# Paired final adds and stores, w1 loaded after all of x, an earlier first spin, and a new rank table in a hedgehog-mixer plus MLP kernel

## The chip, the cores and the metric

The kernel runs on one core of a Trainium2 chip. The metric is the device time of one execution in microseconds, as the median of repeated runs. The engines are TensorE (PE; its weight loads are shown apart as PEld), VectorE (DVE), ScalarE (ACT), GpSimd (POOL) and SyncE (SP). SP computes nothing: it issues nearly all transfers, one after the other.

## The reference, cut to what matters

x is a 2048 x 448 block in bf16 (D = 448, 16 heads of 28, F = 1792).

```python
xn = layernorm(A_x)
# A: linear attention with softmax feature maps
q, k, v = split_heads(xn @ wqkv)
phi(t) = concat(softmax(t @ w_phi), softmax(-(t @ w_phi)))      # per head
o = (phi(q) @ (phi(k).T @ v)) / (phi(q) @ sum_s phi(k) + 1e-6)
A = merge_heads(o) @ wo
# B: token-shift mixer, then an MLP
h  = gelu(layernorm(xn) @ w1)
x1 = xn + concat(4 column blocks of h, shifted by +1, -1, +2, -2 rows) @ w2
B  = x1 + gelu(layernorm(x1) @ w3) @ w4
return A_x + A + B
```

B_x is not read: both branches work on xn.

## The kernel before

The 2048 rows are 16 tiles of 128 rows; tile i holds row `res_of(i)` of each group of 16, so neighbours in time are neighbouring tiles. Everything stays in SBUF. PSUM is four slots of two banks each (pool `ps`); each matmul group takes a slot until it is copied out.

The program is not written in its final order. `P.add(name, engine, cost, rank, deps, emit, uses)` adds a task, and `Planner.run` (L245) lays all tasks out by list scheduling: among the tasks that could start about now on an engine, the one with the lowest rank goes first. The ranks come from a table of text, `RANKS` (L366), read by `set_ranks` (L351); a number after `@` is an earliest start. `Planner.run` also holds an estimate of how long loads take: a task with a negative `lag` waits in one line behind the earlier loads. `Recorder` (L17) then turns the order into one instruction stream for each engine and works out which waits each instruction needs. So a changed rank or cost can move any instruction of any engine, but never changes what is computed. All VectorE and GpSimd work has line L209, all activations L205, matmuls L197, transposes on PE L201, plain transfers L212 and transposing transfers L215.

The tasks, in the order of the work, with the names used below:

- Loads on SP, in the order the table gives: `x0`, `x1`, `x2` (2 tiles), `x4`, `x8`, `x12` (4 tiles each, 448 KB); `wk`, `wq`, `wv`, `w1` in pieces of 336 and 56 KB (L586 to L637). ACT issues `phi`.
- `z_kvq` (L689): seven VectorE memsets of `kvq`. `spin0` to `spin19` (L730): twenty matmuls of 240 columns on `kvq`, whose result nobody reads; each can start when `z_kvq` is done.
- LayerNorm of tile i on VectorE: `st` (statistics), `ag`, `sc..e`, then `sc` on POOL (the power), `ap` (apply) and `du` (a copy of 64 columns).
- `xT0` to `xT3`: tiles 0 to 3 transposed on PE, copied out by `xTc0` to `xTc3`. Tiles 4 to 15 are transposed by transfers `xD4` to `xD15` on SP, each after its `du`.
- `wTk`, `wTq`: 16 transposes each of the K and Q weights, copied out by `wTck0/1`, `wTcq0/1`; then `foldk0/1`, `foldq0/1` multiply them by w_phi, copied out by `foldck0/1` and `foldcq0/1` on ACT.
- `Vj`, `Kj` (j = 0 to 7, two tiles each, 14 matmuls of 448 columns in two parts, a with 8 and b with 6) and `Qn` (n = 0 to 7, 14 matmuls of 512). Each K and Q is followed by two exponentials on ACT (`.e0`, `.e1`), each V by a copy (`.e`) on ACT or VectorE. `red`, `rec`, `nrm` normalise phi(k).
- `W1j` and four `gel` (Gelu) tasks per j on ACT, after the table load behind `warm2`. `nudge0/1` and `put6` to `put9` move four blocks across the edge of the shift. `hDj` (SP) transposes h, `W2j` multiplies by w2, `W2j.r` adds xn; `hD` has three buffers, so hD6, hD5, hD7 wait for W20.b, W21.b, W22.b.
- `kv0` to `kv3`, `kvm`: phi(k).T @ v. `numi` (16 matmuls), `n1` to `n7` and `oDj`: the attention output of tile i, its division and its transpose.
- A second LayerNorm, `gDj` (SP) its transpose, `Hg_f` (g = 0 to 3, f = 0 to 6; 14 matmuls of 512, Gelu `.g` on ACT), and at last `Fp_q`: h3 @ w4 and o @ wo for two tiles, 70 matmuls. `xsi` (POOL) is xn plus x.
- `fini.q` (VectorE) adds `xs` to the F result, `outi.q` stores it (L1237 to L1247): one of each per tile. F7 is cut into two column halves, q = 0 and 1.

Of the kernel before, what the change touches and what calls it, by code (L numbers as in the profile page):

```python
# [366 lines left out]
warm 868.4 tiny 970.5 phi -70.0 x0 -486.0 x1 -79.6 wk0 -291.7 wk1 284.2 x2 326.9 wv0 1117.1 wv1 954.7 wv2 792.3 wq0  # L367
444.5 wq1 375.6 x4 733.3 x8 1139.7 x12 1546.2 w10 640.0 w11 1288.0 w12 1936.1 bdl -321.6 bdh 970.7@5139 mask
1098.4@1625 pick 966.2@4497 ident 958.1@1998 mhalf -318.4 z_h 959.3@1573 nudge 971.2@1597 z_pk -285.0 z_v -272.1 z_wpq
998.3 z_kvq 286.2 st0 853.0 ag0 208.4 sc0e 294.4 sc0 -285.3 ap0 258.7 du0 57.9 st1 204.5 ag1 60.2@4897 sc1e 288.1 sc1  # L370
997.3 ap1 243.1 du1 1112.4 st2 205.2 ag2 227.0 st3 252.9 ag3 294.2 sc2e 1063.7 sc2 970.7 ap2 63.9 ap3 271.9 du2 268.8
st4 84.4 ag4 239.6 st5 239.8 ag5 874.0 sc4e 102.1 sc4 991.8 ap4 286.4 ap5 495.5 du4 65.4 st6 287.4@11185 ag6 865.4 st7
239.4@11166 ag7 156.1 sc6e 205.0 sc6 971.2@13677 ap6 157.0 ap7 220.7 du6 90.4 st8 28.7@13523 ag8 243.2@16614 st9
288.9@13637 ag9 413.8 sc8e -323.1 sc8 1243.7 ap8 782.0@20130 ap9 797.1 du8 1090.5 st10 243.7@13806 ag10 84.0 st11
259.2@13643 ag11 205.1 sc10e 244.0 sc10 986.2 ap10 495.3 ap11 156.9 du10 82.0@20186 st12 313.5 ag12 204.3 st13 761.4
ag13 28.6@20784 sc12e 263.1 sc12 1162.8 ap12 176.8 ap13 157.2 du12 369.7 st14 234.9@18290 ag14 305.3@19922 st15
82.9@17719 ag15 228.5@19848 sc14e 313.4 sc14 1188.5@22933 ap14 251.2 ap15 262.1 du14 264.6 f0 1188.9 f8 870.9@24467
xT0 296.7@6540 xT1 589.9@8454 xTc0 769.9@7438 xTc1 829.3 xT2 308.9 xT3 575.0 xTc2 822.2@11260 xTc3 896.9@11975 xD4
463.2 xD5 487.3 xD6 397.4 xD7 480.3 xD8 479.7 xD9 456.4 xD10 490.4 xD11 488.2 xD12 476.1@27407 xD13 425.8@25657 xD14
422.8@28403 xD15 486.3@30159 wTk 278.3 wTck0 872.2 wTck1 847.2 foldk0 291.2@8902 foldck0 873.4 foldk1 290.8@7999  # L380
foldck1 861.1 wTq 597.2@7001 wTcq0 815.4 wTcq1 576.6 foldq0 112.7@9432 foldcq0 873.8@10814 foldq1 309.8 foldcq1
770.5@11650 V0.a 131.0 V0.b 596.4 V0.e 814.9 V1.a 611.2 V1.b 621.0 V1.e -217.9 V2.a 283.7@19412 V2.b 243.7 V2.e 855.1
V3.a 258.1@25132 V3.b 615.5 V3.e 530.1 V4.a 413.8 V4.b 487.7@32840 V4.e 648.6 V5.a 2130.9 V5.b 315.3 V5.e 343.8 V6.a
1092.4 V6.b 656.1 V6.e 491.9 V7.a 1096.5 V7.b 374.4 V7.e -228.4 K0.a 590.7 K0.b 596.7 K0.e0 875.6 K0.e1 507.0 red0
1501.6 rec0 1501.9 nrm0 1188.1 red1 1498.0@21181 rec1 118.3 nrm1 1157.5 K1.a 283.9@17349 K1.b 609.8 K1.e0 509.1 K1.e1
-216.6 red2 786.6 rec2 515.2 nrm2 1160.2 red3 264.5@32297 rec3 290.1 nrm3 1159.4 K2.a 575.7 K2.b 283.4 K2.e0
-202.6@23116 K2.e1 919.1 red4 797.0 rec4 226.8 nrm4 870.8 red5 1498.8 rec5 293.5 nrm5 407.5@40914 K3.a 183.0 K3.b
621.3 K3.e0 828.9 K3.e1 501.7 red6 1377.0 rec6 499.7 nrm6 399.9@33939 red7 516.5@30012 rec7 1379.7 nrm7 1187.7 K4.a
675.4 K4.b 1438.8 K4.e0 729.0 K4.e1 718.7 red8 1533.4 rec8 1413.5 nrm8 390.6 red9 1380.6 rec9 1474.4 nrm9 407.3 K5.a
644.7@37806 K5.b 683.8 K5.e0 496.9 K5.e1 496.4 red10 1439.5 rec10 -331.0 nrm10 403.0 red11 1435.2@50122 rec11  # L390
-297.4@53022 nrm11 415.4 K6.a 401.9 K6.b 644.6 K6.e0 -263.9@34806 K6.e1 501.3@33944 red12 1500.3 rec12 1437.9 nrm12
857.2 red13 1417.4 rec13 1380.5 nrm13 1159.5 K7.a 682.7 K7.b 1126.1 K7.e0 493.7 K7.e1 648.4 red14 307.4 rec14 1462.0
nrm14 1098.5 red15 1418.2 rec15 1474.5 nrm15 407.1 Q0.a 569.0 Q0.b 263.5 Q0.e0 543.6 Q0.e1 543.6 Q1.a 290.1 Q1.b 596.6
Q1.e0 785.1 Q1.e1 522.7 Q2.a 1491.2 Q2.b 261.5 Q2.e0 647.5@28961 Q2.e1 242.8@28196 Q3.a 595.2 Q3.b 242.4 Q3.e0 785.4
Q3.e1 -312.2 Q4.a 175.1 Q4.b 283.7 Q4.e0 904.2@33049 Q4.e1 498.8 Q5.a 355.3 Q5.b 413.2 Q5.e0 499.2 Q5.e1 903.8 Q6.a
594.9 Q6.b 478.9 Q6.e0 492.2 Q6.e1 529.8 Q7.a 1057.0 Q7.b 683.2 Q7.e0 349.0 Q7.e1 660.7 warm2 529.2@45117 W10.a
656.5@43897 W10.b 949.8 gel0.0 728.6 gel0.1 340.6 gel1.0 532.8 gel1.1 744.8 W11.a 804.7 W11.b 213.9 gel2.0 -228.0
gel2.1 658.3 gel3.0 482.7 gel3.1 659.0 W12.a 916.6 W12.b 930.6 gel4.0 349.8 gel4.1 494.5 gel5.0 519.7 gel5.1 482.9
W13.a 1439.6 W13.b 682.4 gel6.0 640.8 gel6.1 725.6 gel7.0 492.4@53544 gel7.1 493.3@52599 W14.a 1446.7 W14.b 1478.5
gel8.0 644.4 gel8.1 372.5 gel9.0 349.8@55542 gel9.1 494.5 W15.a 1073.7@51311 W15.b 525.8 gel10.0 658.6 gel10.1 656.9  # L400
gel11.0 349.9 gel11.1 350.4 W16.a 2141.1 W16.b 1086.0 gel12.0 358.7 gel12.1 492.6@57478 gel13.0 688.0 gel13.1
366.6@57534 W17.a 687.1 W17.b 707.4 gel14.0 491.3 gel14.1 492.1 gel15.0 366.1 gel15.1 -228.4 nudge0 1075.4@59991 put8
505.8@60597 put9 327.7@61558 nudge1 1073.1 put7 492.5 put6 736.9 hD0 177.9 hD1 147.9 hD2 187.5 hD3 194.4 hD4 213.9 hD5
223.0@59251 hD6 199.2 hD7 198.0@59683 kv0 918.8 kv1 1477.9 kv2 1071.3 kv3 882.5 kvc 1430.0 kvm 259.3 kvo0 1803.8 kvo1
1544.6 w20 485.1 w21 419.6 w22 417.3 w23 525.4 W20.a 1446.5 W20.b 1060.2 W20.r 1493.4 st2_0 1438.4 ag2_0 1431.6 st2_1
1535.3 ag2_1 1020.8@59199 sc2_0e 1487.3 sc2_0 409.9@61475 ga0 1036.1 ga1 1450.3@62958 gD0 187.6 W21.a 214.3 W21.b
523.9 W21.r 1464.6 st2_2 1438.2 ag2_2 1488.1 st2_3 1437.9 ag2_3 1464.8 sc2_2e 1556.8 sc2_2 376.0 ga2 1418.4 ga3 1036.5
gD1 162.3 W22.a 525.7 W22.b 525.6 W22.r 1557.2 st2_4 1535.7@63878 ag2_4 1826.3 st2_5 1750.8 ag2_5 909.6@73450 sc2_4e
1470.9@74052 sc2_4 947.9@75836 ga4 1547.5 ga5 1503.7 gD2 148.3 W23.a 497.9 W23.b 524.6 W23.r 1849.7 st2_6 1900.8 ag2_6
1451.3 st2_7 1813.2 ag2_7 1410.1@73193 sc2_6e 1487.6 sc2_6 857.8 ga6 1036.7 ga7 749.0 gD3 157.7 W24.a 297.4@76488  # L410
W24.b 525.9 W24.r 1874.5 st2_8 1416.0 ag2_8 1033.4 st2_9 1529.3 ag2_9 1721.7 sc2_8e 1548.2 sc2_8 666.0 ga8 743.9 ga9
1943.6 gD4 266.5@86330 W25.a 907.3 W25.b 279.2@65249 W25.r 1518.3@67862 st2_10 1906.4 ag2_10 1504.1 st2_11
1545.7@73156 ag2_11 1739.6@75171 sc2_10e 1901.7 sc2_10 872.0 ga10 1813.1 ga11 749.7@85280 gD5 290.3 W26.a 1070.4 W26.b
465.7@63251 W26.r 1813.1 st2_12 1567.0@67359 ag2_12 1825.8 st2_13 1036.4@66877 ag2_13 1885.8@74867 sc2_12e 1826.4
sc2_12 407.8 ga12 1828.6 ga13 1545.9@100527 gD6 1700.4 W27.a 283.9@66012 W27.b 297.5 W27.r 1503.5 st2_14 1419.6 ag2_14
1437.5@71900 st2_15 1825.9@74052 ag2_15 1548.0 sc2_14e 1548.2@82777 sc2_14 925.1 ga14 746.9@95166 ga15 1904.0 gD7
1685.8 w30 419.0 w31 406.5 wo0 423.1 wo1 491.3 wo2 461.4 w4 494.1 num0 466.2 n1_0 1546.3 n2_0 1393.7 n3_0 1760.0@76183
n4_0 749.2 n5_0 1904.7 n6_0 1069.2 n7_0 936.0 num1 525.7 n1_1 1544.5 n2_1 1896.2 n3_1 1470.5@81970 n4_1 1559.1 n5_1
1776.2 n6_1 1813.2 n7_1 927.9@86239 od0 1946.5 oD0 268.1 num2 504.3@83674 n1_2 1526.8@85094 n2_2 1770.0 n3_2 1039.2
n4_2 989.8 n5_2 1778.7 n6_2 1814.1 n7_2 1695.3 num3 541.1 n1_3 1796.4 n2_3 1722.5 n3_3 1957.9 n4_3 1527.3 n5_3 1001.0  # L420
n6_3 1526.9 n7_3 662.7 od1 1896.2 oD1 293.4 num4 551.0 n1_4 752.3 n2_4 1546.2 n3_4 1901.0 n4_4 748.0 n5_4 2206.7 n6_4
1533.1 n7_4 1772.9 num5 557.6 n1_5 751.8 n2_5 2205.0 n3_5 1021.6 n4_5 1512.8 n5_5 1021.8 n6_5 1596.5 n7_5 598.4 od2
1015.6 oD2 1674.3 num6 841.7 n1_6 1513.0 n2_6 723.9 n3_6 1593.5 n4_6 745.4 n5_6 1010.2 n6_6 1594.1 n7_6 663.6@106936
num7 1026.4 n1_7 2207.5 n2_7 1545.8 n3_7 1545.5 n4_7 2209.9 n5_7 744.5 n6_7 1542.2 n7_7 600.2 od3 1884.4 oD3 1734.2
# [29 lines left out]
def bass_parallel_sum__linear_kernel_hedgehog__mixer_s_mlp__prompt_kernel(  # L454
# [18 lines left out]
    with es:  # L473
# [114 lines left out]
        def load(name, dst, src, rank, eng="SP", kb=100.0, after=()):  # L588
            return P.add(name, eng if isinstance(eng, dict) else {eng: 510}, None, rank, after,
                         lambda t: R.dma(dst, src, t.eng), lag=-kb * RATE.get(name, 2.6 if dst.ap[-1][1] > 512 else 3.3))  # L590
# [691 lines left out]
```

The softmax here doesn't subtract the row's maximum and nothing guards it: scores larger than these inputs give would overflow.

## Time and profile before

| | us |
|---|---|
| median of 13 runs | 178.1 (177.1 to 178.84) |
| the profiled execution | 177.1 |
| its span in the profile | 175.4 |
| PE busy in the span | 169.3 (97%), 2080 matmuls |
| DVE, ACT, POOL busy | 115.1, 81.4, 78.9 |
| transfers | 18.30 MB, mean 104 GB/s |

The profiled execution is the fastest of the 13 runs. What lies between its time and its span (1.7 us) is outside the program's instructions. The first 16 spins take 3.38 us, 0.2 us each, and the 16 transposes of `wTk` after them 2.00 us; the same 16 transposes of `wTq`, from 8.06 us on, take 1.20. The tables of the profile give starts and durations in us from the span's start; "L197 PE MATMUL ps<-w,hT" is a matmul that reads w and hT and writes the tile ps.

The order on SP before is x0 wk0 x1 wk1 x2 wq1 wq0 w10 x4 wv2 wv1 wv0 x8 w11 x12 w12, then the transposes xD.

### The profile page before, as it was taken

To read this page: it belongs to the slowest core of one execution; us is meant where nothing else is said; L and a number is where in the kernel's file an instruction comes from. 1 tells how busy PE (TensorE), PEld (TensorE's weight loads), DVE (VectorE), ACT (ScalarE), POOL (GpSimd) and SP (SyncE) were. 2 spreads that over 40 slices of the span, in tenths; PEclk is the share of its full clock that TensorE was granted. 3 is DMA by queue.
4 is the path that set the end of the run, shared out by engine and by line. 5 is a ranking of instruction groups with operands and counts; after the bars stand their busy time and mean duration, and the time that the engine had idled before them with its cause. 6 is when DMAs were issued, how large, how long until landed. Compare 5 with 4: busy or idle time off the path is not lost.

```text
span 175.4 us, 4846 instructions
## 1 busy us (share of the span) xinstructions
PE 169.3 (97%) x2080; PEld 106.2 (61%) x2080; DVE 115.1 (66%) x300; ACT 81.4 (46%) x116; POOL 78.9 (45%) x105
## 2 busy tenths in 40 slices
PE   5999999999999979999999999999999999999993
PEld 4875555555555655455555667655666666766793
DVE  3889999977991898995986655820654554370133
ACT  3399999989999411173657000427001561200000
POOL 7526387699469034035522254630138141261080
PEclk9999999999999999999999999999999999999999
DMA  6994445599909497523054526130010403313022
GB/s 153 260 343 112 74 82 102 113 390 310 322 8 179 89 103 131 104 51 74 4 111 86 106 39 136 53 64 0 0 56 26 90 0 64 60 52 64 0 86 79
DMA packets 41766, 18.30 MB, mean 104 GB/s; under 512 B 33552, under 2 KB 40848, under 8 KB 41744
## 3 DMA queue, kind: packets, MB, share of 16 engines
q1 hardware_dynamic: 41136, 17.91, 43.3%
q8 instruction: 16, 0.26, 0.6%
q10 hardware_dynamic: 608, 0.08, 0.3%
q14 instruction: 6, 0.05, 0.1%
HBM read 8.28 MB, written 1.84 MB: 58 GB/s over the span
## 4 chain that ended last, share of the span: by engine, by line
PE 92%; DMA 5%; DVE 1%; issue 1%; DVEq 0%; SPq 0%
PE ps L197 90%; DMA hT<-hq 3%; PE ps L201 2%; DMA gT<-wv 2%; DVE kvq L209 0%; DVE vaug L209 0%; DVEq L169 0%; SPq L215 0%
## 5 line engine op out<-in xcount | busy, mean ns | idle before, releaser
L205 ACT ACTIVATE phik<-ps 128x1024 bf16<-128x1024 f32 (+1 forms) x44 | 41.3, 997 | 44.7 <-PE ps L197 44.7
L209 DVE TENSOR_TENSOR vaug<-ps,vaug 128x464 f32<-128x464 f32 (+3 forms) x66 | 32.9, 505 | 21.3 <-PE ps L197 15.9
L197 PE MATMUL ps<-w,phik 64*128 64x448 bf16 (+1 forms) x504 | 46.0, 328 | 0.0
L197 PE MATMUL ps<-gT,w 64*128 64x512 bf16 x392 | 44.5, 376 | 0.3 <-DMA gT<-wv 0.3
L197 PEld LDWEIGHTS ps<-w,phik 64*128 64x128 bf16 x504 | 29.5, 94 | 12.2 <-ACT phik L205 0.3
L197 PEld LDWEIGHTS ps<-gT,w 64*128 64x128 bf16 x392 | 22.8, 94 | 17.5 <-DVE vaug L209 0.7
L209 POOL TENSOR_TENSOR xnT<-vaug 128x224 bf16<-128x224 f32 x32 | 17.3, 565 | 27.7 <-DVE vaug L209 27.7
L209 POOL TENSOR_TENSOR vaug<-xn,xtok 128x448 f32<-128x448 bf16 x16 | 16.5, 1039 | 28.6 <-DVE vaug L209 26.4
L209 POOL TENSOR_TENSOR phik<-phik,ksum 128x896 bf16<-128x896 bf16 x14 | 25.0, 1813 | 6.2 <-DVE ksum L209 6.2
L209 POOL TENSOR_TENSOR rs<-rs,mhalf 128x2 f32<-128x2 f32 (+1 forms) x17 | 11.5, 685 | 28.3 <-DVE rs L209 21.1
L205 ACT ACTIVATE eq<-ps 120x1024 bf16<-120x1024 f32 (+1 forms) x18 | 17.5, 1043 | 5.9 <-PE ps L201 5.0
L209 DVE TENSOR_REDUCE ksum<-phik 128x32 f32<-128x896 bf16 x16 | 16.7, 1063 | 1.5 <-ACT phik L205 1.5
L209 DVE RECIPROCAL vaug<-ps 128x16 f32<-128x16 f32 x16 | 4.1, 254 | 19.1 <-PE ps L197 19.1
L197 PE MATMUL ps<-wo,xnT 64*128 64x448 bf16 (+1 forms) x126 | 14.1, 328 | 0.0
L197 PE MATMUL ps<-xnT,hq 64*120 64x512 bf16 x112 | 13.4, 376 | 0.0
L197 PE MATMUL ps<-wv,xnT 64*128 64x448 bf16 x112 | 13.2, 349 | 0.0
L197 PE MATMUL ps<-w,hT 64*128 64x448 bf16 x56 | 12.1, 349 | 1.0 <-DMA hT<-hq 1.0
L197 PE MATMUL ps<-wpk,xnT 64*128 64x448 bf16 x112 | 12.9, 349 | 0.0
L197 PE MATMUL ps<-w2s,hT 64*128 64x448 bf16 x56 | 12.1, 350 | 0.0
L209 DVE TENSOR_TENSOR xn<-ps,xn 128x896 bf16<-128x896 f32 x8 | 8.5, 1076 | 5.0 <-PE ps L197 4.9
L205 ACT ACTIVATE hq<-ps,fs 128x224 bf16<-128x224 f32 x32 | 11.1, 497 | 0.2
L197 PE MATMUL ps<-w,xnT 64*128 64x448 bf16 x112 | 11.1, 349 | 0.0
(71 smaller groups left out, 170.0 us busy)
## 6 DMA issues: line engine op xcount, KB each, us to landing
w<-in_B_w_dram SPq DMA_DIRECT2D x2, 896.0 KB, 6.8
w<-in_B_w_dram SPq DMA_DIRECT2D x1, 1568.0 KB, 12.1
out_dram<-vaug SPq DMA_DIRECT2D x14, 112.0 KB, 1.7
xtok<-in_A_x_dram SPq DMA_DIRECT2D x3, 448.0 KB, 6.4
eq<-in_A_wqkv_dram SPq DMA_DIRECT2D x2, 336.0 KB, 3.6
w<-in_B_w_dram SPq DMA_DIRECT2D x2, 336.0 KB, 6.6
wv<-in_A_wqkv_dram SPq DMA_DIRECT2D x1, 336.0 KB, 5.5
w2s<-in_B_w_dram SPq DMA_DIRECT2D x1, 336.0 KB, 5.3
```

The costliest lines, as they stand in the source:

```text
L197: self.op("PE", lambda e: e.matmul(out, lhsT, rhs, start=start, stop=stop, skip_group_check=True), [out], [lhsT, rhs], after=after)
L201: self.op("PE", lambda e: e.transpose(out, in_, ident), [out], [in_, ident])
L205: self.op("ACT", lambda e: e.activation(out, in_, func, **kw), [out], [in_] + aps)
L209: self.op(eng, lambda e: getattr(e, name)(out, *args, **kw), [out], aps)
```

## The change

Four edits, and a new table of ranks for all tasks.

1. `fin` and `out` handle two tiles at once: one VectorE instruction of 128 x 2 x 448 elements (2 x 224 for F7's halves) and one store. There are 9 of each instead of 18. An access pattern over both banks of the PSUM slot and over the two buffers is built by `rows`.
2. `w1`'s three loads come after all loads of x, and the planner's estimate of load times is one rate, 3.8 ns per KB (3.0 for the large ones), in place of 3.3, 2.6, 4.0 and 5.4.
3. The first memset of `kvq` is cut in two: `z_spin` clears the first 120 of 240 words, and the spins wait for it alone; `z_kvq` does the rest.
4. The table `RANKS` is replaced as a whole, so the order changes nearly everywhere.

```diff
 RANKS = """
-warm 868.4 tiny 970.5 phi -70.0 x0 -486.0 x1 -79.6 wk0 -291.7 wk1 284.2 x2 326.9 wv0 1117.1 wv1 954.7 wv2 792.3 wq0
+warm -327.6 tiny -301.4 phi -70.0 x0 -355.2 x1 -220.2 wk0 -6.9 wk1 -209.6 x2 -85.2 wv0 106.3 wv1 115.8 wv2 125.4 wq0
...
-        RATE = {"x2": 5.4, "x4": 4.0, "x8": 2.6, "x12": 2.6}
+        RATE = {"x8": 3.0, "x12": 3.0, "w10": 3.0, "w11": 3.0, "w12": 3.0}
...
-                         lambda t: R.dma(dst, src, t.eng), lag=-kb * RATE.get(name, 2.6 if dst.ap[-1][1] > 512 else 3.3))
+                         lambda t: R.dma(dst, src, t.eng), lag=-kb * RATE.get(name, 3.8))
...
+        z_spin = P.add("z_spin", dve, 350, -31, [], lambda t: R.ew(dve, "memset", kvq[:, 0:1, :, :], 0.0))
+
         def kvq_ones(t):
-            R.ew(dve, "memset", kvq[:, :, :, :], 0.0)
+            R.ew(dve, "memset", kvq[:, 1:2, :, :], 0.0)
...
-        z_kvq = P.add("z_kvq", dve, 900, -30, [], kvq_ones)
+        z_kvq = P.add("z_kvq", dve, 900, -30, [z_spin], kvq_ones)
...
-                z = kvq.rearrange("p s c n -> p (s c n)")
+                z = kvq[:, 0, :, :].rearrange("p c n -> p (c n)")
...
-            P.add("spin%d" % n, "PE", 102, 2000, [z_kvq], spin, [("ps", "spin")], mode=128)
+            P.add("spin%d" % n, "PE", 102, 2000, [z_spin], spin, [("ps", "spin")], mode=128)
...
-                    for d, i in enumerate((i0, i1)):
-                        def fin(t, k=k, d=d, i=i, u=u, v=v):
-                            R.ew(dve, "tensor_tensor", outb[:, P.slot[("ob", i)], u:v], bank(P.slot[k], d)[:, 0:v - u],
-                                 xs[:, P.slot[("xs", i)], u:v], op=ALU.add)
...
+                    def rows(view_, p, i0=i0, i1=i1, u=u, v=v):
+                        a, b = (P.slot[(p, i)] for i in (i0, i1))
+                        return bass.AP(view_.tensor, view_.offset + D * a + u, [list(view_.ap[0]), [D * (b - a), 2], [1, v - u]])
+
+                    def fin(t, k=k, i0=i0, i1=i1, u=u, v=v, rows=rows):
+                        R.ew(dve, "tensor_tensor", rows(outb, "ob"), both(P.slot[k])[:, :, 0:v - u], rows(xs, "xs"), op=ALU.add)
...
+                    def stor(t, i0=i0, u=u, v=v, rows=rows):
+                        R.dma(outr[:, res_of(i0):res_of(i0) + 2, u:v], rows(outb, "ob"), t.eng)
```

The order that comes out, where it matters below (before, then after):

```
SP   before  x0 wk0 x1 wk1 x2 wq1 wq0 w10 x4 wv2 wv1 wv0 x8 w11 x12 w12 | xD4 xD5 xD6 xD7 xD11 xD9 xD8 xD10 ...
SP   after   wq0 x0 wq1 x1 wk1 x2 wk0 x4 wv0 wv1 wv2 x8 x12 w10 w11 w12 | xD5 xD4 xD7 xD6 xD8 xD10 xD11 xD9 ...
PE   before  spin x16, wTk, 2 spins, xT0, spin, wTq, spin, foldk1 xT1 foldk0 foldq1 foldq0 xT2 xT3 K0.a V0.a K0.b V0.b Q1.a Q0.a ...
PE   after   spin x18, wTq, 2 spins, wTk, xT1 foldq1 xT0 foldq0 foldk1 foldk0 V0.a xT2 xT3 V0.b K0.a Q1.a K0.b Q0.a ...
PE   before  W22.b kv0 nudge1 nudge0 kv1 W26.a kv2 W25.a W26.b kv3 W25.b W27.a kvm W27.b W23.a num0 W23.b H0_3.a ...
PE   after   W22.b kv0 nudge0 nudge1 kv1 W26.a W25.a W26.b W25.b kv2 W27.a kv3 W27.b W23.a kvm W23.b W24.a H0_0.a ...
ACT  before  wTck1 xTc0 wTcq0 foldck1 foldck0 foldcq0 foldcq1 xTc2 xTc3 K0.e1 V0.e K0.e0 Q1.e1 ...
ACT  after   wTcq0 wTcq1 wTck0 foldcq1 foldcq0 foldck0 foldck1 xTc2 V0.e K0.e1 K0.e0 Q1.e0 ...
```

The matmuls are the same 2080 in both.

## Prediction

> **What bounds the kernel now.** I read the chain of waits in order of time first, then the busy time of each engine by stage, then the timeline of the start and the issue-to-landing times of single transfers.
>
> ```profile
> 12.17 46.04 PE ps L197 x469
> 58.21 5.03 DMA hT<-hq
> ...
> 68.54 3.29 DMA gT<-wv
> 71.83 0.25 issue
> 72.08 100.50 PE ps L197 x1262
> 172.58 0.38 DVE vaug L209
> ```
>
> Start, length, what. TensorE carries the chain except for two transposes that it waits for.
>
> ```profile
> 4.35:8.06 3.71, 3.69 (x28) 3.04 (x27) 3.06 (x11) 0.97 (x2) 2.45 (x8) 1.00 0.91 241
> 8.06:12.10 4.04, 4.04 (x69) 3.48 (x70) 3.33 (x11) 3.42 (x5) 0.70 (x1) 1.00 1.03 353
> ...
> 17.78:44.80 27.02, 27.02 (x276) 14.76 (x274) 24.23 (x52) 26.45 (x31) 20.74 (x16) 1.00 0.69 184
> ...
> 60.05:72.08 12.03, 10.70 (x209) 6.89 (x208) 11.15 (x25) 1.87 (x5) 3.42 (x4) 1.00 0.88 138
> 72.08:172.56 100.48, 100.48 (x1276) 65.21 (x1276) 54.43 (x155) 28.20 (x31) 35.69 (x52) 1.00 0.25 55
> ```
>
> Busy us of PE, PEld, DVE, ACT, POOL in each stretch, then clock, DMA share, GB/s. From 8.06 to 172.56 PE stands idle only in the stretch 60.05 to 72.08: 12.03 - 10.70 = 1.33 us (1.05 for hD6, 0.29 for gD1). From 17.78 to 44.80 ACT is busy for 26.45 of 27.02 us, so it is nearly as tight. As the matmuls stay the same, only four things can move the end: when the dense part begins, those 1.33 us, new holes, and the 2.8 us of the tail.
>
> ```profile
> 1.88 3.38 PE L197 MATMUL ps<-kvq 128*128 128x240 bf16 x16 [1.88 <-DVE kvq L209]
> 8.06 1.20 PE L201 MATMUL ps<-ident,eq 128*112 128x128 bf16 x16
> 9.19 0.92 ACT L205 ACTIVATE eq<-ps 112x896 bf16<-112x896 bf16 x1 [0.61 <-PE ps L201]
> 172.56 0.69 DVE L209 TENSOR_TENSOR vaug<-ps,vaug 128x224 bf16<-128x224 f32 x2 [0.79 <-PE ps L197]
> ```
>
> The start is gated at 8.06 by the second weight to be transposed (wTq). The transfer behind it, issued at 3.98, took 4.0 us:
>
> ```profile
> eq<-in_A_wqkv_dram SPq DMA_DIRECT2D x1, 336.0 KB, 4.0
> ```
>
> **The earlier spin.** z_kvq's first memset takes 0.26 us for 240 words from 0.91; for 120 words I take half (bounds 0.07, a small memset's row, and 0.26). Spins then begin near 1.15 instead of 1.88. 18 of them at 0.2 us end at 4.75; wTq at the slow rate takes 1.93 (5.05 to 6.98, wTk's row), to 6.7; two spins, to 7.1. After that PE has nothing until wk0 is there. So the gain is nothing: it is hidden by that wait. The cover's price if it is gone: 0.73 us, the whole shift.
>
> The rows show slow matmuls up to 7.8 (0.2 us per spin) and fast ones from 8.06. [...]
>
> **The loads, and the start of the dense part.** In both orders the same seven loads (x0, x1, x2, wk, wq; 1,232 KB) come before the second weight is whole; w1 comes only later. Before, the last of them landed at 3.98 + 4.0 = 8.0. After, wk0 is also the seventh issue, near 3.9. Upper bound 3.9 + 4.0 = 7.9, with PE at 8.0; lower bound 3.9 + 3.2 (wk0's own row when it was second), but not before the spins' end, so 7.3. The large wq0 first in line fills the transfer engines where x0 (112 KB) did not; I take 7.8, that is 0.25 before 8.06.
>
> From that moment I add PE's own steps by their start-to-start times. Before, from 8.06: wTq 1.13, spin 0.11, foldk1 0.61, xT1 0.24, foldk0 0.39, foldq1 0.61, foldq0 0.41, xT2 and xT3 0.54, K0 and V0 2.66: 6.70, to 14.76. After: the same, without the spin (-0.11), with xT0, which before lay in the slow part (+0.24), and with two more changes between 128- and 64-row mode around xT2 and xT3 (0.08 each): 6.99. ACT's five copies of 0.82 each end where K0.a needs them (start plus 1.13, 5 x 0.82 and 0.3 of waits for PE: 5.5, against 5.7 when PE is there), so PE sets it. Net: +0.29 - 0.25 = **+0.05**, bounds -0.5 and +0.35. The x tiles land about 1.4 us sooner without w10 in front (336 KB: 9.55 against 8.02 for the load before it), but the first statistics of tiles 4 and 5 now stand behind VectorE's weight copy, so nothing on the path gains.
>
> **Up to the W2 groups.** K0.b is now third, not first, among the second parts, so ACT's first exponential begins about 1.6 us later (14.40 against 16.0), of which it recovers most: V0.e is done before and xTc3 has gone to VectorE. By 32 exponentials (0.81 each for K, 0.91 for Q) and two copies I get ACT's last at about +0.2 us. PE keeps a slot's lead of 0.1 to 0.5 us at each group: no hole, by little.
>
> **The 1.33 us.** hD6, which waits for one of hD's three buffers, came 5.0 us after issue, where its first three siblings took 3.2:
>
> ```profile
> hT<-hq SPq DMA_TRANSPOSE x1, 5.0
> ```
>
> In the window 61.0 to 62.2 the transfer view shows why:
>
> ```profile
> q1 hardware_dynamic: 371, 0.09, 214.3%
> q8 instruction: 1, 0.02, 4.8%
> ```
>
> A 16 KB instruction fetch (16 of them in the page, 0.26 MB) starts at 61.20, and the transposes' packets all but stop until 62.9. It feeds TensorE's stream, so it comes at a fixed place of it, at the first matmuls of kv1, and the same matmuls stand before that place in both orders. hD6's other wait, Gelu 30 of 32, is the same too. So I leave this 1.05 us where it is (bounds: 0, if hD6 lands before the fetch; 1.3, if later).
>
> [...]
>
> gD1's 0.29 goes: W24 (1.32 us of PE work) now stands before H0 in part (W24.a, 0.76), while gD1 is issued at much the same 68.5. What is late next: hD3, issued behind W26.b at 65.9, is now in flight when the next fetch comes (about 68.0, before W27's end); at 2.05 us after the fetch's start it holds W23.a for 0.2. Sum of this stage: **-0.1** (bounds -1.3 and +0.5).
>
> **Paired fin and out.** Each pair saves one instruction's overhead: two of 224 columns took 0.69, one of 448 takes 0.62. Hidden behind PE in seven pairs of nine, and the pair frees its PSUM slot no later than the second of two did. At the end it counts: -0.07. The last store is 112 KB in place of two concurrent ones of 56: medians 1.7 against 1.6, +0.1. Sum 0 (bounds -0.1, +0.4, twice the pieces on one queue). xs of both tiles is now needed at once; POOL has 8 us idle before the last three, which is the cover.
>
> **Sum.** +0.05 - 0.1 + 0 = about -0.1 on a span of 175.4 and a time of 177.1. That execution was the fastest of 13; the median lies 1.0 above it. I carry the difference over: 178.1 - 0.1 = **178.0**.
>
> **Rivals.**
> Case B, slower: a late transpose at Q2.a. Before, xD6 and xD7 landed at 20.9 and 22.3 for K3.a at 23.08. After, du6 on VectorE comes near 18.9 (wTck1 9.1, then the rows' steps), xD7 goes first, xD6 is issued at 20.2 and lands at 22.7, with Q2.a at 23.2. A fetch began at 23.30, and the transpose in flight then took this long, against 2.4 for others:
>
> ```profile
> xnT<-xn SPq DMA_TRANSPOSE x1, 4.0
> ```
>
> If du6 is over 0.5 us later than I work out, xD6 is caught and lands 2.05 after the fetch, near 25.4: a hole of 2.1, 180.1. For it: the margin is half of what it was, and VectorE has no idle time there to recover. Against it: all of VectorE's steps are known rows.
>
> Case D, slower: PE is idle from 7.1 to 7.8, the clock does not rise, and the 4.7 us of fold and transpose work runs at the rate of wTk (2.0 against 1.2): +1.2, 179.3. Against it: before, 5.9 busy us were enough.
>
> Case C, faster: wk0 lands at 7.2 and hD6 beats the fetch: -0.5 - 0.8 - 0.1, 176.7. For it: hD6 missed by only 0.26 us (58.21 + 3.25 against 61.20). Against it: all that comes before moves together.
>
> **Chances.** The sum as worked out: 0.42; C 0.20; B 0.25; D 0.13. What a measurement of this kernel tells from no change is 0.3%, 0.53 us: 177.57 to 178.63. The likeliest case's own range, 177.3 to 178.7, gives 0.12 faster, 0.22 same, 0.08 slower. With C all faster and B and D all slower: faster 0.32, same 0.22, slower 0.46. The range for 8 in 10 is 176.8 to 180.1, most of C and of B.
>
> **What would show it.** wTk's first matmul at 7.3 to 8.0; PE without idle time from there to W26.a; hD6's landing about 2 us after a fetch; H0's first matmul near 72.5 with W24.a done; one last fin of about 0.62. I am wrong if PE idles before Q2.a, if wTk's transposes take 2.0, or if PE's idle time after 60 falls below 0.5.

## The result, and the profile after

| | before | after |
|---|---|---|
| median, us | 177.91 (177.1 to 180.6, 48 runs) | 179.06 (178.69 to 179.77, 11 runs) |
| the profiled execution | 177.1 | 178.77 |
| its span | 175.4 | 176.6 |

The change makes the kernel slower: the ratio is 1.0064, with a 95% interval of 1.0049 to 1.0079, or about 1.15 us. (A ratio leaves out executions more than 1.5% above the fastest of their kernel, here three of the 48.) The forecast was 178.0, no real change. The two profiled executions differ by 1.67 us, since that of before was the fastest of its kind, 0.81 below its median, and that of after lies 0.29 below its own.

The chain of waits of the changed kernel (start, length, what):

```profile
63.22 2.38 PE ps L197 x23
65.60 4.96 DMA hT<-hq
...
70.70 102.56 PE ps L197 x1292
...
173.28 0.62 DVE vaug L209
```

The step by way of gT, which stood ahead of H0, is gone, as foreseen. In its place W23.a waits for hD3, which is in flight for 4.96 us. PE's two idle stretches in the timeline (start, length, then idle before and its releaser):

```profile
63.22 0.35 PE L197 MATMUL ps<-w,hT 64*128 64x448 bf16 x1 [0.47 <-DVE wv L209]
...
70.70 0.35 PE L197 MATMUL ps<-w,hT 64*128 64x448 bf16 x1 [1.00 <-DMA hT<-hq]
```

The first is W26.a. The profile names VectorE for it (a step of the second LayerNorm, which ends at 63.11), and so its chain has no hD6. But W26.a begins 0.14 us after hD6 has landed (63.08), the same 0.14 as before the change and as W23.a behind hD3, and in `a_unpair`, where hD6 was early, it begins at 63.52, ahead of the end of that VectorE step (63.62). So it is hD6 that W26.a waits for.

The busy times by stage (busy us of PE, PEld, DVE, ACT, POOL, then clock, DMA share, GB/s):

```profile
8.00:12.00 4.00, 4.00 (x70) 3.27 (x71) 3.97 (x15) 3.95 (x6) 0.70 (x1) 1.00 0.98 307
...
60.05:72.08 12.03, 10.56 (x192) 6.65 (x190) 11.10 (x26) 1.00 (x5) 3.56 (x5) 1.00 0.98 147
```

From 8 to 12 PE is dense and at full clock, and it stays dense up to the W2 groups. The idle time is in the same stage as before: 12.03 - 10.56 = 1.47 us (0.47 at W26.a, 1.00 at W23.a), against 1.33. The start of PE's timeline (start, length, then idle before and its releaser):

```profile
1.89 3.78 PE L197 MATMUL ps<-kvq 128*128 128x240 bf16 x18 [1.89 <-DVE kvq L209]
5.46 1.93 PE L201 MATMUL ps<-ident,eq 128*112 128x128 bf16 x16
...
7.83 1.20 PE L201 MATMUL ps<-ident,eq 128*112 128x128 bf16 x16
```

The spins still begin at 1.89. The points at which the two executions can be compared, from the starts and landings of the tasks:

| | before | after | difference |
|---|---|---|---|
| kv0 begins (the same PE tasks stand ahead of it) | 60.05 | 60.47 | +0.42 |
| W26.a begins, after its wait for hD6 | 63.38 | 63.22 | -0.16 |
| PE's last matmul ends | 172.56 | 173.25 | +0.69 |
| the last store has landed | 174.87 | 175.74 | +0.87 |
| the span ends | 175.36 | 176.59 | +1.23 |
| the execution's time | 177.1 | 178.77 | +1.67 |

So the 0.42 that PE is late at kv0 costs nothing (the hole ahead of W26.a swallows it), 0.85 is lost between W26.a and PE's end, and 0.98 comes after PE has finished. Of these 0.98 only 0.18 lies before the last store's landing; from that landing to the end it takes 178.77 - 175.74 = 3.03 us, where it took 177.1 - 174.87 = 2.23. The transfer queues of the page, before and then after, show what else is new there (queue, packets, MB, share):

```profile
q14 instruction: 6, 0.05, 0.1%
```

```profile
q14 instruction: 4, 0.03, 0.1%
```

These are instruction fetches of 8 KB each (6 in 0.05 MB, beside 16 of 16 KB on q8); runs below try which engine they go with. Before, the last two begin at 167.9 and 170.8, under PE's last matmuls. After, there is none in that place, but one at 176.89, after the last store and 0.3 us after the span's end. In the window 176 to 177 of the changed kernel it is the only packet:

```profile
q14 instruction: 1, 0.01, 3.1%
```

### The profile page after: what moved, and what is told of

Read it like the earlier page. It is cut to its first block, busy times and chain, and to the rows that moved or that the text cites. A ratio compares the mean times of both kernels' runs of the same rounds, so it can differ in the third digit from the quotient of the medians.

```text
span 176.6 us, 4819 instructions
## 1 busy us (share of the span) xinstructions
PE 169.7 (96%) x2080; PEld 106.8 (60%) x2080; DVE 112.8 (64%) x293; ACT 81.2 (46%) x115; POOL 77.0 (44%) x105
## 4 chain that ended last, share of the span: by engine, by line
PE 88%; DMA 5%; DVE 3%; SPq 2%; issue 0%
PE ps L197 86%; DMA hT<-hq 3%; DMA eq<-in_A_wqkv_dram 2%; SPq L212 2%; DVE xn L209 2%; PE ps L201 1%; DVE st L209 1%; DVE wv L209 0%; DVE vaug L209 0%; DVE mv L209 0%; DVE rs L209 0%
## 5 line engine op out<-in xcount | busy, mean ns | idle before, releaser
L209 DVE TENSOR_TENSOR vaug<-ps,vaug 128x464 f32<-128x464 f32 (+3 forms) x57 | 31.4, 558 | 27.9 <-PE ps L197 24.7
L197 PE MATMUL ps<-gT,w 64*128 64x512 bf16 x392 | 45.2, 376 | 0.0
L197 PEld LDWEIGHTS ps<-w,phik 64*128 64x128 bf16 x504 | 30.2, 94 | 12.2
L209 POOL TENSOR_TENSOR phik<-phik,ksum 128x896 bf16<-128x896 bf16 x14 | 23.3, 1700 | 1.6 <-DVE ksum L209 1.6
L205 ACT ACTIVATE eq<-ps 120x1024 bf16<-120x1024 f32 (+1 forms) x19 | 18.3, 1017 | 4.8 <-PE ps L201 4.6
L197 PE MATMUL ps<-xnT,hq 64*120 64x512 bf16 x112 | 14.4, 377 | 0.0
L209 DVE BATCH_NORM_STATS2 st<-xtok 128x6 f32<-128x448 bf16 x16 | 9.4, 612 | 3.2 <-DMA xtok<-in_A_x_dram 3.2
```

Source lines behind the costliest of these rows:

```text
L197: self.op("PE", lambda e: e.matmul(out, lhsT, rhs, start=start, stop=stop, skip_group_check=True), [out], [lhsT, rhs], after=after)
L205: self.op("ACT", lambda e: e.activation(out, in_, func, **kw), [out], [in_] + aps)
L209: self.op(eng, lambda e: getattr(e, name)(out, *args, **kw), [out], aps)
```

## The experiments

For the runs that keep an order, the planner's result (each task with its engine and its buffer) was written out as a list and played back, so that one edit doesn't move the rest:

```diff
-        P.set_ranks(RANKS)
-        P.run()
+        P.replay(ORDER, SLOTS)
```

### Pairs of final adds and stores

The changed kernel with one `fin` and one `out` per tile again, in its own order (`a_unpair`):

```diff
-                    def fin(t, k=k, i0=i0, i1=i1, u=u, v=v, rows=rows):
-                        R.ew(dve, "tensor_tensor", rows(outb, "ob"), both(P.slot[k])[:, :, 0:v - u], rows(xs, "xs"), op=ALU.add)
...
+                    for d, i in enumerate((i0, i1)):
+                        def fin(t, k=k, d=d, i=i, u=u, v=v):
+                            R.ew(dve, "tensor_tensor", outb[:, P.slot[("ob", i)], u:v], bank(P.slot[k], d)[:, 0:v - u],
+                                 xs[:, P.slot[("xs", i)], u:v], op=ALU.add)
...
```

> The changed kernel in its own order, but every final add and store cut into one per tile again, the last two stores on two queues. Theory 2 with the larger last store's 0.18: faster by 0.6 to 1.0, 178.1 to 178.5. Rival (pairing costs nothing, as predicted): 178.9 to 179.2.

Measured: 178.34 (177.84 to 179.95, 12 runs), ratio to before 1.0036 [1.0015, 1.0057]. That is 0.72 us below the changed kernel's median, within what was expected. By the two ratios it is 0.50 us, with intervals that leave between 0 and 1.

The kernel before with pairs, in its own order (`b_pair`): the same lines the other way round, and xs made for two tiles at a time, because its pool has two buffers:

```diff
-POOL: xs5 xs0 xs1 xs3 xs2 ...
+POOL: xs0 xs1 xs2 xs3 xs4 xs5 ...
```

> The kernel before in its own order, but with final adds and stores in pairs (xs tiles two at a time). Theory 2: slower by 0.5 to 0.9, 178.5 to 178.8. Rival (pairing costs nothing, as predicted): 177.9 to 178.1.

Measured: 178.92, ratio 1.0068 [1.0044, 1.0092], 1.1 us slower, 0.1 above the expected range. Here some 0.35 belong to the way it was built: fin14.1 waits for xs15, which has to wait for the pair before it (2.85 us from PE's end to the last landing, against 2.50 in the changed kernel).

To tell the larger store from the length of the instruction streams, extra waits on events that are long past were put into the changed kernel, which do nothing but fill the instruction streams up to their old length (`a_pad`; `a_pads` on SP alone, `a_padd` on VectorE alone):

```diff
+PAD = {'SP': 10, 'DVE': 13, 'POOL': 3, 'ACT': 2}
...
+                if todo and seen and left and n >= FROM[eng]:
+                    e.wait_ge(get(seen[0]), seen[1])
+                    left -= 1
```

> The changed kernel with extra waits on events long past, so that SP, DVE, POOL and ACT each have as many instructions as before the change (91, 327, 122, 124 in place of 82, 314, 119, 122). Theory 2 (with fewer instructions an 8 KB instruction fetch of one of these engines falls behind the last store, at 176.89, and lengthens the stretch from the last store's landing to the end from 2.2 to 3.0 us): the fetch is back inside the span, 178.3 to 178.8, and time minus last landing about 2.2 to 2.5. Rival (that stretch is the larger last store's, or noise): 179.1 and 3.0.

> The changed kernel with nine extra waits on SP alone (91 instructions there, as before the change; VectorE stays at 314). If the fetch that falls behind the last store is SP's: it is back inside the span, and the time less the last store's landing is 2.2. If it is VectorE's: 3.0.

> The changed kernel with thirteen extra waits on VectorE alone (327 instructions, as before the change; SP stays at 82). If the late fetch is VectorE's: time less the last store's landing is 2.2. If it is SP's: 3.0.

From the last landing to the end of the span, and from there to the end of the execution, in us:

```
            instructions       landing to   span's end   together
            SP     VectorE     span's end   to the time
before      91     327         0.49         1.74         2.23
a_unpair    91     330         0.49         1.72         2.22
a_pad       91     327         0.49         1.73         2.22
a_pads      91     314         0.49         2.16         2.65
a_padd      82     327         0.85         1.81         2.66
after       82     314         0.85         2.18         3.03
b_pair      82     314         0.85         2.09         2.94
```

Both answers of the last two expectations are half right: both streams count. With nine SP instructions fewer the span ends 0.36 us later after the last landing; with thirteen VectorE instructions fewer the stretch behind the span is 0.43 longer. The two add up to 0.8. The seven traces that are not in the table agree with it: 2.21 to 2.26 together where stores are one per tile, 2.95 and 3.01 with pairs. Nor is it the profiled execution alone: from the span's end to the time it takes 2.16 us on average in the twelve executions of the changed kernel and 1.73 in the six of `a_pad`.

In the window 176 to 178 the run with SP filled up has no packet at all, and the run with VectorE filled up has one:

```profile
q14 instruction: 1, 0.01, 1.2%
```

It begins at 177.04, and another is back at 167.8. So one 8 KB fetch stands behind the end with 82 SP instructions (176.89 in the changed kernel, 177.04 here) and not with 91 (before, `a_unpair`, `a_pads`): it is put down to SP. The one near 168 is put down to VectorE: it is there with 327 VectorE instructions (167.9 before, 167.8 here) and not with 314 (the changed kernel, `a_pads`). That these fetches are what takes the time is not shown. SP's 0.36 us lie at the branch that follows its wait for the last store: from there to its next instruction it takes 0.47 to 0.48 us in the five traces with the short SP stream and 0.17 to 0.18 in the nine others. The late packet begins only 0.3 us after the span's end, a full microsecond after that branch (175.83 and 176.89 in the changed kernel). Where the fetch put down to VectorE goes the trace doesn't hold. The larger store is the rest of the pair's price: 2.50 us from PE's end to the last landing with pairs (after, `a_pad`), 2.24 to 2.31 without (`a_unpair`, before): 0.2. The time of `a_pad` itself, 178.91, ratio 1.0047 [1.0029, 1.0066], misses its range by 0.1; its end is shorter by 0.8, but in the profiled execution V1.a also began at 18.83 instead of 17.88, for loads that came later. So the medians show only 0.15 of the 0.8 (0.3 by the ratios, whose intervals overlap). The two short runs, of one time each, are 178.43 (`a_pads`) and 178.56 (`a_padd`).

So the traces show one place where a fetch goes with lost time, beside a transposing transfer (hD3, 4.96 us in flight in the changed kernel and 3.4 in `u_early`, below), and perhaps a second, the 0.36 and 0.43 us at the end of the program.

### The order before and after kv0

The PE tasks ahead of kv0 are the same in both kernels, so the two orders can be crossed there. `ab` takes the changed order up to kv0 and the old one after it, `ba` the other way round; both have unpaired stores:

```diff
 ab, PE: spin x18, wTq, 2 spins, wTk, xT1 ... W22.b
-kv0 nudge0 nudge1 kv1 W26.a W25.a W26.b W25.b kv2 W27.a kv3 W27.b W23.a kvm W23.b W24.a H0_0.a ...
+kv0 nudge1 nudge0 kv1 W26.a kv2 W25.a W26.b kv3 W25.b W27.a kvm W27.b W23.a num0 W23.b H0_3.a ...
```

> The changed kernel's order up to kv0 (loads, weights, K, V, Q, W1: the same tasks as before the change stand ahead of it), then the order of the kernel before; final adds and stores one per tile. Theory 3 (the front costs nothing, because W26.a waits for hD6 either way; the new order after kv0 costs, by hD3's hold): as the kernel before, 177.6 to 178.2. Rival (the front costs, by loads and by 0.4 us up to kv0): as the changed kernel with unpaired stores, 178.2 to 178.6.

> The other half: the order before the change up to kv0, then the changed kernel's order, final adds and stores one per tile. Theory 3: as the changed kernel with unpaired stores, 178.2 to 178.7, and W23.a held for hD3 by 0.7 to 1.0. Rival (the front costs): as the kernel before, 177.6 to 178.1.

| ratio to before | old order after kv0 | new order after kv0 |
|---|---|---|
| old order up to kv0 | 1 | 1.0031 [1.0010, 1.0052] (`ba`, 178.28) |
| new order up to kv0 | 0.9977 [0.9953, 1.0001] (`ab`, 177.51) | 1.0036 [1.0015, 1.0057] (`a_unpair`) |

The new order after kv0 costs 0.3% in one row and 0.6% in the other, 0.5 to 1.0 us; the new front costs nothing and may gain a little (0.9977, an interval that just touches 1; 177.51 is 0.1 below the expected range). In `ba` the chain of waits has hD6's and hD3's transfers, the two that hold PE in the changed kernel, though the front is the old one:

```profile
58.25 4.84 DMA hT<-hq
...
65.59 4.88 DMA hT<-hq
```

PE waits 0.85 us for the first and 0.92 for the second. In `ab` neither is held: hD6 takes 3.04 us and hD3 3.27, for which W23.a still waits 0.75.

### What holds the transposing transfers

The 16 fetches of 16 KB on q8 begin 94 to 162 matmuls apart before the change and 95 to 153 after it. If they belong to places of PE's stream, they can be moved against the work by putting more or fewer instructions ahead of it. `a_shift` has ten spins of 480 columns in place of twenty of 240:

```diff
-        SPIN = 20
+        SPIN = 10
-                R.mm(bank(P.slot[("ps", "spin")], 0)[:, 0:240], z[:, 0:128], z[:, 0:240], True, True)
+                R.mm(bank(P.slot[("ps", "spin")], 0)[:, 0:480], z[:, 0:128], z[:, 0:480], True, True)
```

> The changed kernel with its order kept, but 10 spins of 480 columns in place of 20 of 240: the same PE time in 20 fewer PE instructions, so every later instruction fetch of PE comes at about 20 instructions later in the work (near 61.6 in place of 61.06 and 69.1 in place of 68.54). Theory 1 (a transpose in flight when a fetch starts is held, and hD3 is held so): hD3 lands at 68.7 instead of 70.56 and the 1.0 us that PE waits ahead of W23.a goes; hD6 lands within 0.1 of the fetch and may be free too (0.47 more); gD1 may cost 0.2. Time 177.6 to 178.3. Rival (hD3 is late for its place in SP's queue or for traffic, not for the fetch): 179.1, with W23.a still held for 1.0.

Measured: 179.24, ratio 1.0068 [1.0043, 1.0093]; inconclusive. hD6 was free (3.04 us in flight, no hole ahead of W26.a, but 0.39 ahead of W25.a for hD5), but not hD3 (4.60; W23.a waits 0.63). The loads were late in this execution and hD3 was issued 0.73 us later, while the fetch moved by 0.52: 2.72 us after the issue instead of 2.94, and still in the way. Nor is the place as fixed as assumed: the fetch began when 753 matmuls had started in the changed kernel and 736 here. The shift was too small for the question. So it was made three times as large and in the other direction, on the changed order with unpaired stores (`u_early`) and on the kernel before (`b_early`):

```diff
-        SPIN = 20
+        SPIN = 50
-                R.mm(bank(P.slot[("ps", "spin")], 0)[:, 0:240], z[:, 0:128], z[:, 0:240], True, True)
+                R.mm(bank(P.slot[("ps", "spin")], 0)[:, 0:96], z[:, 0:128], z[:, 0:96], True, True)
```

> The changed kernel's order with unpaired stores, and 50 spins of 96 columns in place of 20 of 240: 60 more PE instructions ahead, so PE's fetches come some 30 matmuls sooner in the work, near 60.0 and 67.4 in place of 61.7 and 69.1. Theory 1 (the fetch holds hD3): hD3 lands by 69.5 in place of 71.2, W23.a is not held, 0.9 us less than with unpaired stores alone: 177.2 to 177.8. Rival (the hold is of another kind): W23.a still held for 0.9, 178.2 to 178.6.

> The kernel before with 50 spins of 96 columns in place of 20 of 240, its order kept. Theory 1: the fetch near 61.2 comes at about 59.5, hD6 (issued 58.2) lands by 61.6 in place of 63.2 and the hole of 1.05 us ahead of W26.a goes; gD0 or gD1 may be held in its place and give up to 1.0 back: 176.9 to 177.9. Rival: W26.a still waits for hD6 by about 1.0, 177.9.

Measured: `u_early` 177.07, ratio 0.9957 [0.9938, 0.9976], 1.27 us below `a_unpair` (1.4 by the ratios), 0.1 below the expected range and faster than both kernels; `b_early` 177.48, ratio 0.9978 [0.9958, 0.9998]. The chain of waits of `a_unpair` has two transfers of hT (hD5's and hD3's); that of `u_early` has none:

```profile
20.07 3.46 DMA xnT<-xn
...
57.65 11.31 PE ps L197 x200
...
69.03 3.14 DMA gT<-wv
...
72.31 100.04 PE ps L197 x1269
```

and PE has no idle time left in the stage where it had 1.47 us in the changed kernel and 1.28 in `a_unpair` (0.35 ahead of W25.a, 0.93 ahead of W23.a):

```profile
60.05:72.08 12.03, 12.03 (x210) 7.44 (x205) 11.94 (x28) 2.02 (x6) 3.65 (x5) 1.00 0.86 154
```

hD3's issue to landing, in the changed kernel and in `u_early` (the fetch now begins 0.66 us after the issue instead of 2.94):

```profile
hT<-hq SPq DMA_TRANSPOSE x1, 5.0
```

```profile
hT<-hq SPq DMA_TRANSPOSE x1, 3.4
```

In `b_early` the hole of 1.05 us ahead of W26.a is gone and W23.a waits 0.35 in its place. The first line of the chain of `u_early` is a small price: a fetch at 20.96 now meets xD6, which takes 3.46, and Q2.a waits 0.39. H0 waits another 0.18 for gD1. By the traces alone the gain over `a_unpair` is 1.28 - 0.39 - 0.18 = 0.7 us; where the rest of the 1.27 comes from stays open.

### The start

The spins on a tile of their own, so that they really begin early (`a_spin`):

```diff
-        z_spin = P.add("z_spin", dve, 350, -31, [], lambda t: R.ew(dve, "memset", kvq[:, 0:1, :, :], 0.0))
+        z_spin = P.add("z_spin", dve, 350, -31, [], lambda t: R.ew(dve, "memset", zsp[:, :], 0.0))
...
-                z = kvq[:, 0, :, :].rearrange("p c n -> p (c n)")
+                z = zsp
```

> The changed kernel with the spins on a tile of their own, which VectorE clears first, so that they can start when that one memset is done and not after z_kvq: first spin near 1.1 to 1.2 in place of 1.89. The prediction's step on the earlier spin: the gain is hidden by the wait for wk0 (7.8), 178.8 to 179.3. Rival: TensorE's start counts, 0.4 to 0.75 less, 178.3 to 178.6.

Measured: a median of 180.24, ratio 1.0092 [1.0059, 1.0126]; a miss of both expectations. In 6 of its 10 executions TensorE's mean granted clock was 0.978 to 0.99 (0.996 or more in all of the changed kernel, 0.998 or more in 73 of 74 executions of the kernel before that were measured beside these runs), and these took 180.2 to 182.5; the four at 1.0 took 178.4 to 179.3, as the changed kernel. The profile of one of the six shows why (PE's timeline, then the stages as above):

```profile
1.10 3.78 PE L197 MATMUL ps<-zsp 128*128 128x240 bf16 x18 [1.10 <-DVE zsp L209]
...
9.36 2.04 PE L201 MATMUL ps<-ident,eq 128*112 128x128 bf16 x16 [2.99 <-DMA eq<-in_A_wqkv_dram]
```

```profile
8.00:12.00 4.00, 2.64 (x23) 2.44 (x24) 1.57 (x9) 0.75 (x1) 0.70 (x1) 0.57 0.94 300
12.00:18.00 6.00, 6.00 (x70) 4.17 (x69) 4.36 (x15) 4.26 (x7) 0.70 (x1) 0.72 0.41 141
```

The spins do begin at 1.10 and end 0.8 us sooner. Then PE stands idle for 2.99 us until wk0 is there (late in this execution), and the transposes of wTk take 2.04 instead of 1.20. The granted clock is 1.00 up to 8.57 us, 0.50 from there to 15.40 and 1.00 after it; the 0.57 and 0.72 above are means over it. From 4 to 12 us PE was idle for 2.99 us here and for 2.54 in the profiled execution of `best1` below, where the clock fell too; in that of `b_early` it was idle for 1.53, and the clock stayed at 1.00. How much idle time it takes, and over what stretch, was not tried.

At last `u_early` with this tile for the spins and with wk0 loaded ahead of wk1 and x2 (`best1`):

```diff
-SP: wq0 x0 wq1 x1 wk1 x2 wk0 x4 ...
+SP: wq0 x0 wq1 x1 wk0 wk1 x2 x4 ...
```

> The changed order with unpaired stores and 50 short spins, as in the run that was faster than both kernels, and two more edits at the start: the spins on a tile of their own, and wk0 loaded ahead of wk1 and x2. If the start is what TensorE now waits for, wTk begins 0.4 to 0.9 sooner (near 6.9 to 7.4) and the time falls by 0.3 to 0.8 from 177.1: 176.3 to 176.8. Rival: wv's loads or the statistics of tile 0 and 1 end the next wait and nothing is left: 177.0 to 177.3.

Measured: 179.56, ratio 1.0041 [1.0008, 1.0074], a miss to the other side. wTk did begin at 6.90, but x2 came later, and VectorE's st3 waited for it (8.25, against 6.71 in `u_early`) with ap1 of tile 1 queued behind. So PE waited 1.65 us for xT1 (9.75, against 8.88), and the clock was 0.95 from 8 to 12 and 0.75 from 12 to 18 (0.50 from 11.59 to 15.01). In 8 of the 12 executions the mean clock was 0.99 or less; the four others took 177.5 to 178.2, still above `u_early`. The two edits were not tried apart. `u_early` is the fastest version of this study.

## Why the prediction was wrong, point by point

- **Earlier spin, worth nothing.** The sum was right, the course was not. Spin0 waits for all of z_kvq, as before: z_kvq's memsets of ones write words that the spins read, they stand ahead of the spins in the planner's order, and Recorder derives the wait from the bytes, whatever dependency the task names. The edit does nothing to the spins (1.89, after 1.88). Where it is made to do what it says, the gain is hidden by the wait for wk0, as worked out, as long as the clock holds; where the clock fell (to 0.50 for 6.83 us in the profiled execution, after 2.99 us of idle time), 1.2 to 3.4 us were lost. Case D named this price (wTk's transposes at 2.0), but for a clock that has not risen by then; in `a_spin` it was 1.00 from 5.16 to 8.57 and then fell. The changed kernel has neither: its clock is 1.00 from 7.19 on, ahead of wTk.
- **Start, +0.05.** Right: wTk at 7.83 (forecast 7.8), V1.a at 17.88 against 17.78: +0.10. But from execution to execution V1.a moved between 17.5 and 19.0 with one and the same order of loads on SP (`ba`, `b_pair`), more than what was worked out. The measured time of wk0 or wv0 in one profile is one draw. The reason given for the 7.8 does not show: with wq0 first in line the DMA share from 2.0 to 2.7 us is 0.52, against 1.08 before.
- **Up to the W2 groups, no hole; case B.** Right: xD6 landed at 22.63, ahead of the fetch at 24.5, and Q2.a began at 23.18 without a wait. Not foreseen: W20.a and W20.b now stand side by side, and the second begins 0.22 late; why is not shown. Nothing of it counts, since W26.a waits for hD6 either way.
- **The 1.33 us, -0.1.** The mechanism was right at both places: hD6 is held by the first fetch (61.06, landing 63.08, 4.71 us after its issue), gD1's wait goes, hD3 is caught by the next (4.96). The size of the last was not, and here the step failed: "it holds W23.a for 0.2" came from a fetch at 68.0; it came at 68.54, and PE was ready for W23.a 0.2 sooner than worked out. Nor was the place of a fetch in PE's stream fixed, as the step took it to be: the one near 61 began with 632 matmuls started before and 619 after. The hold was 1.00, and 0.49 to 0.95 in the six other traces with this order after kv0 and 10 or 20 spins behind the new front. The new order after kv0 costs 0.5 to 1.0 us by the crossed runs, where -0.1 stood.
- **Paired fin and out, 0 (bounds -0.1, +0.4).** This step failed too: undoing the pairs gained 0.5 to 0.7 us. Its terms were about right as far as they went: 0.62 us for the last add, and 0.2 for the larger store where 0.1 stood. What it put at nothing is the length of the streams: nine SP and thirteen VectorE instructions fewer make the end of the program 0.36 + 0.43 = 0.8 us longer in the traces, and filling the streams up again takes that back. The step counted the instructions as cost alone and not as positions in a stream, although the page of before had the 8 KB fetches at 167.9 and 170.8, four to eight us from the end.
- **From the span to the median.** The difference of 1.0 was carried over from the fastest execution. After the change the stretch behind the span is itself 0.44 longer, which no span shows.

Put together, by the times: the pairs 0.5 to 0.7, the order after kv0 0.5 to 1.0, the front 0 to -0.4, that is 0.6 to 1.7 against 1.15 measured. By the traces the pairs alone come to 0.8 + 0.2 = 1.0; why the times show less of it stays open, and so does how much of the front's gain is chance.

None of the three signs by which the prediction said it would be wrong appeared: PE did not idle ahead of Q2.a, wTk's transposes took 1.20, and PE's idle time after 60 was 1.47. Its chance of 0.46 for "slower" stood for cases B and D, neither of which came. That the time still lies within its wide range is luck.

## What to carry to other kernels

An instruction is also a position in a stream (here 60 more PE instructions ahead of the work were worth 1.27 us, and nine SP and thirteen VectorE instructions fewer cost 0.8 at the end of the traces): when some are removed or added, look where the page's instruction fetches stand against the transfers that the bottleneck engine waits for, and how long the program takes to end. Compare time less last landing, and not spans alone. And where idle time hides an edit at the start, the clock may be what the idle time costs, as in `a_spin` (0.50 for 6.83 us).

## What the hardware showed that was not expected

In these traces the time of a transposing transfer goes with when PE's 16 KB fetch (q8) begins after its issue. For hD6, hD3 and gD0 over all fourteen:

```
fetch begins, us after the issue   issue to landing, us      transfers
-0.2 to 0.7, or no fetch           3.0 to 3.5                19
2.49 to 2.56                       3.04 to 3.11, one 4.45    8
2.67 to 2.99                       4.5 to 5.0                15
```

This looks like a sharp edge, but for these three no fetch began between 0.7 and 2.49. All the 336 transposes of h, of the second LayerNorm and of o in the fourteen traces fill the gap (some of them were in flight together with a held one):

```
fetch begins, us after the issue   issue to landing, us      transfers
none from -1.0 to the landing      3.0 to 3.4                161
-1.0 to -0.3                       3.0 to 3.8                35
-0.3 to 0.75                       3.0 to 4.4                47
0.75 to 2.3                        3.8 to 4.6                36
2.3 to 3.05                        3.0 to 3.3                23
2.3 to 3.05                        4.4 to 5.0                25
3.05 to 3.35                       3.0 to 3.2                9
```

A fetch that began 0.75 to 2.3 us after the issue lengthened every transfer (36 of them, 3.8 to 4.6 us against 3.0 to 3.4). One at the issue cost between nothing and 1.4 us. Of those from 2.3 on, 25 cost 1.4 to 2.0 and 32 nothing, and the offset alone does not tell which: at 2.49, hD3 was held in `a_padd` and hD6 was free in `a_shift`; at 2.67, a transpose of o was held in `u_early` and another was free in `b_early`. Why was not tried.
